# A spectral token mixer: the first transform takes h with rescaled constants, ScalarE copies its whole bank, and the first rows are reordered

## The chip, the cores and the metric

The kernel runs on one core of one Trainium2 chip. The metric is the device time of one execution in microseconds. The core's engines each work through a queue of their own, in order: TensorE (PE, with its weight loads shown apart as PEld), VectorE (DVE), ScalarE (ACT), GpSimd (POOL) and SyncE (SP), which here only issues loads and stores. They meet at semaphores.

## The reference

With x of 2048 tokens by 512 channels, all in float32:

```python
xn = _layernorm(x, axis=-1)
s = _A_ref(xn, A_w_r, A_w_i)      # irfft2(rfft2(xn) * (w_r + 1j * w_i))
g = _silu(_B_ref(xn, B_w1, B_b1, B_w2, B_b2))
return x + s * g
```

`_B_ref` normalises xn once more to h, and mixes the tokens of each channel: gelu(h^T w1 + b1) w2 + b2, with 1792 hidden units, transposed back. So one branch is a two-dimensional spectral filter, the other a token MLP, and the gated product is added to x.

## The kernel before

The 2048 tokens lie as 16 rows of 128 (token 16p + j is partition p of row j), so that row j is one 128x512 tile. The work falls into three stages: up to about 107 us the rows are normalised, the first half of the hidden units is accumulated, and the first transform is made; up to about 217 us the other half of the hidden units and the filter; then w2, the inverse transforms and the output. The change lies in the first stage, in a loop over j from 0 to 15.

**What a row needs.** The mean and the variance of each token come from `stats` and `spreads` (L165, L175, L169, L170), a square root on ScalarE (L171), and `scales` (L179 to L183), which end in `nb`, the bias with which ScalarE makes h. Rows are done in pairs: one set of these small operations serves two rows, except at rows 0 and 1, which have sets of their own. There are two scales for each token, columns 0 and 1 of `rs`: the first makes xn of x, the second makes h of x directly, for the second normalisation of an already normalised token is one more scale.

- h (L186, ScalarE, `normed`) is split into a high part `hh` (L311, `high`, ScalarE) and the remainder `hl` (L314, `low`, VectorE), so that a product in float32 becomes three products of rounded parts. Rows of w1 are split in the same way, 4 blocks of 128 units (`w1h`, `w1l`, 128x512) and 3 blocks (128x384).
- PE then adds 7 x 3 products of 512 columns to banks 0 to 6 (L319, `hidden_early`).
- xn (L189, VectorE, `normed_v`) goes through the first transform: 4 products with the constants `cf` (L197, `first_transform`) into bank 7, between the second and the third group of row products. The tokens of the row are the contracted dimension.
- `first_copy` (L202) brings the second half of bank 7 to SBUF, and `fold` adds and subtracts the first half from PSUM (L207, L208), makes the combinations `t` (L210, L211), moves half of `o` to the other partitions by ScalarE (L215), and writes `ey` by VectorE (L218) and POOL (L213, L214).

**What sets the order.** Operations within `keep(...)` stay on their engine in the order in which the program writes them; this holds for all that VectorE and ScalarE do in this loop. PE's, POOL's and SP's instructions are placed by the scheduler. In iteration j the program writes row j's products, then the preparation of row j + 1 (h, splits), then the fold of row j, and in even iterations the moments of rows j + 2 and j + 3, so that ScalarE and VectorE work one row ahead of PE. In ScalarE's queue the copy of o (L215) of row j stands directly ahead of h of row j + 2.

**Buffers.** h has one buffer, xn two, x five; raw w1 three in each of its two pools. SP issues the loads in the order written, except where a load must wait for a buffer or a queue.

Of the kernel before, what the change touches and what calls it, by code (L numbers as in the profile page):

```python
# [15 lines left out]
P = 128  # L16
# [90 lines left out]
def spectral_mixer_kernel(tc, x, w1, b1, w2, b2, wk, we, wx, c_f, c_ft, c_d, c_i, c_g, c_h, out):  # L107
# [14 lines left out]
    with tc.tile_pool(name="ps", bufs=1, space=PSUM) as psp, ExitStack() as left, ExitStack() as right:  # L122
# [28 lines left out]
        def load_x(j):  # L151
            xs[j] = lnp.tile([P, D], F32, name=f"x{j}", tag="x", bufs=5)
            SY.dma_start(xs[j], x[:, j])
# [3 lines left out]
        def moments(nm, n):  # L157

            return {k: lnp.tile([P, 2, w], F32, name=f"{k}{nm}", tag="m" + k, bufs=3)[:, :n]
                    for k, w in (("st", 6), ("mv", 2), ("v2", 2), ("sd", 2), ("r0", 2), ("t", 2), ("rs", 2), ("nb", 1))}

        def stats(m, i, src):
            keep(V.bn_stats(m["st"][:, i], src))  # L165
# [12 lines left out]
        def scales(m):  # L178
# [4 lines left out]
            keep(V.scalar_tensor_tensor(m["nb"], m["mv"][:, :, 0:1], -1.0, m["rs"][:, :, 1:2], op0=ALU.mult, op1=ALU.mult))  # L183

        def normed(dst, src, m, i):
            keep(A.activation(dst, src, AF.Identity, bias=m["nb"][:, i], scale=m["rs"][:, i, 1:2]))  # L186
# [4 lines left out]
        def new_h(j):  # L191
            return lnp.tile([P, D], F32, name=f"h{j}", tag="h", bufs=1)

        def first_transform(xn):
            z = ps[:, 7].rearrange("p (b c) -> p b c", c=P)
            for b in range(4):
                T.matmul(z[:, b], xn[:, b * P:(b + 1) * P], cf, start=True, stop=True)  # L197
            return z

        def first_copy(j, z):  # L200
            zt = lnp.tile([P, 2, P], F32, name=f"zt{j}", tag="zt")
            keep(A.activation(zt, z[:, 2:4], AF.Copy))  # L202
            return zt

        def fold(j, z, zt):
            e, o, t = (lnp.tile([P, w, P], F32, name=f"{n}{j}", tag=n) for n, w in (("e", 2), ("o", 2), ("t", 1)))
            yield keep(V.tensor_sub(o, z[:, 0:2], zt))  # L207
            yield keep(V.tensor_add(e, z[:, 0:2], zt))  # L208

# [91 lines left out]
        raws = {(0, 0): w1_load(0, *WA)}  # L301
        SY.dma_start(cf, c_f)
        load_x(1)
        raws[0, 1] = w1_load(0, *WB)
        for j in range(2, 5):
            load_x(j)
        for _ in range(WARM):
            T.matmul(ps[:, 0], wz[:, :P], wz, start=True, stop=True)

        def high(dst, src):  # L310
            keep(A.activation(dst, src, AF.Copy))  # L311

        def low(dst, src, hi):
            keep(V.tensor_sub(dst, src, hi.bitcast(F32)))  # L314
# [10 lines left out]

        def new_xn(j):
            return lnp.tile([P, D], F32, name=f"xn{j}", tag="xn")

        m = moments("m0", 2)
# [5 lines left out]
        w = w1_tiles(0, *WA), w1_tiles(0, *WB)  # L335
        h, xn = new_h(0), new_xn(0)
# [16 lines left out]
        folds = iter(())  # L353
        for j in range(NJ):
            more = j + 1 < NJ
            if more:
                raws[j + 1, 0], raws[j + 1, 1] = w1_load(j + 1, *WA), w1_load(j + 1, *WB)
            if j == 0:
                SY.dma_start(b1t, b1)
                SY.dma_start(b2t, b2)  # L360
                G.dma_start(cft, c_ft)
            if j == 4:
                SY.dma_start(cd, c_d)
            if j in (6, 8, 10, 12):
                q = slice(16 * (j - 6), 16 * (j - 4))
                SY.dma_start(out[q, :NJ - 1], x[q, :NJ - 1])
            z = hidden_early(j, 4, 0, w[0], lambda: first_transform(xn))
            hidden_early(j, 3, 4, w[1], lambda: None)
            if more:
                w = w1_tiles(j + 1, *WA), w1_tiles(j + 1, *WB)  # L370
                h, xn = new_h(j + 1), new_xn(j + 1)
# [12 lines left out]
            if j + 3 < NJ:  # L384
# [394 lines left out]
```

## Time and profile before

| | |
|---|---|
| time, median of 3 runs | 400.4 us (400.11 to 401.9) |
| profiled execution | 400.3 us, its span 398.5 us |
| PE busy, share of span | 387.5 us, 97% |
| DVE | 333.9 us, 84% |
| ACT | 238.4 us, 60% |
| POOL | 49.3 us, 12% |
| first stage | 0 to about 107 us |

The span runs from the first to the last instruction that the profiler saw; 1.8 us of the profiled execution lie around it. A busy share counts time in which an engine has an instruction in work, and matmuls are pipelined with modelled ends, so PE's share says little on whether PE sets the pace. What an engine waited for, and which instruction ended the wait, is read from the groups of instructions and from the chain of waits, which follows the last instruction back from releaser to releaser. In its rows stand the start in us, the length in us, the engine, the tile and the line.

### The profile page before, as it was taken

The page shows a single profiled execution, that of the slowest core. Times are in us where ns is not written, and L with a number is a line of the kernel's source. Part 1 is how long each engine was busy: PE and PEld are TensorE (multiplying, and loading weights), DVE is VectorE, ACT ScalarE, POOL GpSimd, SP SyncE. Part 2 cuts the span into 40 slices and gives each one's busy share as a digit, 9 for nine tenths or more (in the row PEclk, how much of TensorE's full clock was granted, in tenths as well). Part 3 has the DMA queues.
Part 4 walks back from the last instruction along what each step waited for, and adds up shares of the span by engine and source line. Part 5 has one row for each costly group of instructions (what it writes and reads, how often), then busy time and mean ns, then how long its engine had stood idle before and what let it go on. Part 6 is the DMA issues. An engine that isn't in the chain of part 4 may idle for free.

```text
span 398.5 us, 7090 instructions
## 1 busy us (share of the span) xinstructions
PE 387.5 (97%) x2456; PEld 337.5 (85%) x2456; DVE 333.9 (84%) x792; ACT 238.4 (60%) x439; POOL 49.3 (12%) x90
## 2 busy tenths in 40 slices
PE   8989999999999999999999999999999999999995
PEld 4677777778877878787878889999999999999995
DVE  5888888988789989998889599888887878787964
ACT  3445444455887875678775677474746465655552
POOL 1111212212200000000000101221210211020200
PEclk9999999999999999999999999999999999999999
DMA  7836344721563645566344839979787878795602
GB/s 249 286 127 200 118 158 159 259 66 39 139 204 128 184 130 172 157 174 177 115 126 146 211 102 260 204 222 178 215 162 204 149 217 147 213 157 156 117 16 53
DMA packets 35080, 64.72 MB, mean 162 GB/s; under 512 B 4194, under 2 KB 19426, under 8 KB 34916
## 3 DMA queue, kind: packets, MB, share of 16 engines
q1 hardware_dynamic: 30436, 52.86, 42.7%
q0 software_dynamic: 4608, 11.41, 17.5%
q8 instruction: 19, 0.31, 0.3%
q14 instruction: 17, 0.14, 0.1%
HBM read 60.05 MB, written 8.13 MB: 171 GB/s over the span
## 4 chain that ended last, share of the span: by engine, by line
PE 69%; DVE 17%; ACT 6%; DMA 5%; issue 2%; SPq 1%; DVEq 0%; ACTq 0%; POOLq 0%
PE ps L717 33%; PE ps L119 6%; PE ps L118 6%; PE ps L120 6%; PE ps L319 4%; PE ps L652 4%; PE ps L421 3%; PE ps L429 3%; DVE w1l L314 3%; PE ps L480 3%; ACT h L186 2%; DMA s<-in_w_dram 2%; DMA w1r<-in_w_dram 2%; DVE stm L165 2%; DVE h L314 2%
## 5 line engine op out<-in xcount | busy, mean ns | idle before, releaser
L319 PE MATMUL ps<-h,w1h 128*128 128x512 f32 x224 | 60.7, 402 | 2.4 <-ACT h L311 2.0
L319 PEld LDWEIGHTS ps<-h,w1h 128*128 128x128 f32 x224 | 40.6, 189 | 12.6 <-ACT h L311 3.6
L118 PE MATMUL ps<-h,w1h 128*128 128x512 f32 x112 | 50.4, 451 | 0.1
L596 DVE TENSOR_TENSOR w2f<-s,w2f 128x896 fp32r<-128x896 f32 x32 | 34.9, 1092 | 17.7 <-ACT w2f L595 17.0
L120 PE MATMUL ps<-h,w1l 128*128 128x512 f32 x112 | 45.3, 404 | 0.0
L119 PE MATMUL ps<-h,w1h 128*128 128x512 f32 x112 | 44.3, 395 | 0.0
L717 PE MATMUL ps<-fa,w2f 128*128 128x256 f32 x336 | 43.1, 281 | 0.0
L717 PE MATMUL ps<-fb,w2f 128*128 128x256 f32 x336 | 42.8, 281 | 0.1
L717 PE MATMUL ps<-fc,w2f 128*128 128x256 f32 x336 | 41.4, 280 | 0.9 <-DVE fc L258 0.9
L717 PEld LDWEIGHTS ps<-fa,w2f 128*128 128x128 f32 x336 | 41.2, 188 | 0.8 <-DVE w2f L596 0.2
L717 PEld LDWEIGHTS ps<-fb,w2f 128*128 128x128 f32 x336 | 40.8, 188 | 0.7 <-DVE c L687 0.5
L717 PEld LDWEIGHTS ps<-fc,w2f 128*128 128x128 f32 x336 | 40.0, 188 | 1.3 <-DVE fc L258 1.1
L595 ACT ACTIVATE w2f<-s 128x896 fp32r<-128x896 f32 x32 | 30.2, 949 | 15.9 <-DVE s L609 11.2
L319 PE MATMUL ps<-h,w1l 128*128 128x512 f32 x112 | 31.4, 394 | 0.0
L596 DVE TENSOR_TENSOR w2f<-a,w2f 128x896 fp32r<-128x896 f32 x24 | 26.1, 1086 | 5.4 <-ACT w2f L595 5.4
L595 ACT ACTIVATE w2f<-a 128x896 fp32r<-128x896 f32 x24 | 22.8, 949 | 11.2 <-PE ps L717 7.9
L586 POOL DMA_DIRECT2D s<-in_w_dram x16 | 13.8, 861 | 115.3 <-DMA s<-in_w_dram 44.3
L314 DVE TENSOR_TENSOR w1l<-w1r,w1h 128x512 fp32r<-128x512 f32 (+1 forms) x32 | 19.8, 620 | 9.0 <-ACT w1h L311 9.0
L118 PEld LDWEIGHTS ps<-h,w1h 128*128 128x128 f32 x112 | 21.2, 189 | 6.3 <-issue 2.6
L119 PEld LDWEIGHTS ps<-h,w1h 128*128 128x128 f32 x112 | 21.2, 189 | 5.6 <-issue 2.6
L120 PEld LDWEIGHTS ps<-h,w1l 128*128 128x128 f32 x112 | 21.0, 188 | 5.4 <-issue 1.0
L319 PEld LDWEIGHTS ps<-h,w1l 128*128 128x128 f32 x112 | 21.0, 188 | 4.9
(123 smaller groups left out, 776.0 us busy)
## 6 DMA issues: line engine op xcount, KB each, us to landing
a<-in_w_dram SPq DMA_DIRECT2D x24, 448.0 KB, 3.8
wt<-in_wk_dram SPq DMA_DIRECT2D x16, 512.0 KB, 3.7
s<-in_w_dram SPq DMA_DIRECT2D x16, 448.0 KB, 4.3
s<-in_w_dram POOLq DMA_DIRECT2D x16, 448.0 KB, 6.5
w1s<-in_w_dram SPq DMA_DIRECT2D x48, 128.0 KB, 2.7
w1r<-in_w_dram SPq DMA_DIRECT2D x16, 256.0 KB, 4.0
x<-in_x_dram SPq DMA_DIRECT2D x15, 256.0 KB, 3.1
out_dram<-in_x_dram SPq DMA_DIRECT2D x4, 960.0 KB, 7.9
```

Of the source, the lines that this page charges most:

```text
L118: T.matmul(o, lh, rh, start=first, stop=False)
L119: T.matmul(o, lh, rl, start=False, stop=False)
L120: T.matmul(o, ll, rh, start=False, stop=last)
L314: keep(V.tensor_sub(dst, src, hi.bitcast(F32)))
L319: T.matmul(ps[:, bank + i], w[wi][:, i * P:(i + 1) * P], hj, start=first and j == 0, stop=last and j == NJ - 1)
L421: T.matmul(pd[:, b * P:(b + 1) * P], eyl[:, b], cd[:, b], start=True, stop=True)
L429: T.matmul(px, gf, sh, start=True, stop=True)
L586: G.dma_start(t, w2_half(*added), accum_op=ALU.add)
L595: A.activation(wf[:, 0], v, AF.Copy)
L596: V.tensor_sub(wf[:, 1], v, wf[:, 0].bitcast(F32))
L652: T.matmul(pe[:, b % 2, b // 2], yt[:, b], ci[:, b], start=True, stop=True)
L717: T.matmul(o, wf[:, wi, i], ui, start=m + a == 0 and n in (1, 2, 5), stop=m == NH - 1 and a == 2, skip_group_check=n in (6, 3, 7, 4))
```

## The change

xn is no longer made. The two scales of a token differ by a factor q, which is the first scale over the second; POOL computes it as `rs0 * rs1 * v2` by two small multiplications per set of scales. Since the tokens are the contracted dimension, xn's transform is h's with row p of the constants multiplied by q of token p: ScalarE makes such constants for each row (`turned`, 128x128), and the transform takes h and these. For rows from 2 on the program writes the transform ahead of the row's products. `first_copy` takes the whole bank, and the fold reads SBUF alone. h gets two buffers, t one. On ScalarE the high part of h now comes ahead of w1h, then the constants, the copy of z, and the smaller w1h. At the start, row 1's statistics stand within row 0's preparation, x of row 1 is loaded ahead of the constants, x of rows 3 and 4 behind w1 of row 1, and the load of cft is written in iteration 4.

```diff
-                    for k, w in (("st", 6), ("mv", 2), ("v2", 2), ("sd", 2), ("r0", 2), ("t", 2), ("rs", 2), ("nb", 1))}
+                    for k, w in (("st", 6), ("mv", 2), ("v2", 2), ("sd", 2), ("r0", 2), ("t", 2), ("rs", 2), ("nb", 1),
+                                 ("q", 1))}
...
+            G.tensor_mul(m["q"], m["rs"][:, :, 0:1], m["rs"][:, :, 1:2])
+            G.tensor_mul(m["q"], m["q"], m["v2"][:, :, 1:2])
+
...
         def new_h(j):
-            return lnp.tile([P, D], F32, name=f"h{j}", tag="h", bufs=1)
-
-        def first_transform(xn):
+            return lnp.tile([P, D], F32, name=f"h{j}", tag="h")
+
+        def turned(j, m, i):
+
+            c = lnp.tile([P, P], F32, name=f"cf{j}", tag="cfj")
+            keep(A.activation(c, cf, AF.Copy, scale=m["q"][:, i]))
+            return c
+
+        def first_transform(h, c):
             z = ps[:, 7].rearrange("p (b c) -> p b c", c=P)
             for b in range(4):
-                T.matmul(z[:, b], xn[:, b * P:(b + 1) * P], cf, start=True, stop=True)
+                T.matmul(z[:, b], h[:, b * P:(b + 1) * P], c, start=True, stop=True)
             return z
...
-            zt = lnp.tile([P, 2, P], F32, name=f"zt{j}", tag="zt")
-            keep(A.activation(zt, z[:, 2:4], AF.Copy))
+            zt = lnp.tile([P, 4, P], F32, name=f"zt{j}", tag="zt")
+            keep(A.activation(zt, z, AF.Copy))
             return zt
...
-            e, o, t = (lnp.tile([P, w, P], F32, name=f"{n}{j}", tag=n) for n, w in (("e", 2), ("o", 2), ("t", 1)))
-            yield keep(V.tensor_sub(o, z[:, 0:2], zt))
-            yield keep(V.tensor_add(e, z[:, 0:2], zt))
+            e, o, t = (lnp.tile([P, w, P], F32, name=f"{n}{j}", tag=n, bufs=w) for n, w in (("e", 2), ("o", 2), ("t", 1)))
+            yield keep(V.tensor_sub(o, zt[:, 0:2], zt[:, 2:4]))
+            yield keep(V.tensor_add(e, zt[:, 0:2], zt[:, 2:4]))
...
         raws = {(0, 0): w1_load(0, *WA)}
-        SY.dma_start(cf, c_f)
         load_x(1)
         raws[0, 1] = w1_load(0, *WB)
-        for j in range(2, 5):
-            load_x(j)
+        SY.dma_start(cf, c_f)
+        load_x(2)
...
         normed(h, xs[0], m, 0)
+        m1 = moments("m1", 1)
+        stats(m1, 0, xs[1])
         low(w[0][1], raws[0, 0], w[0][0])
+        spreads(m1, 1)
         high(w[1][0], raws[0, 1])
-        normed_v(xn, xs[0], m, 0, 0)
+        c = turned(0, m, 0)
         low(hl[0], h, hh[0])
+        scales(m1)
         low(w[1][1], raws[0, 1], w[1][0])
-        m = moments("m1", 1)
-        stats(m, 0, xs[1])
-        spreads(m, 1)
-        scales(m)
-        of = {1: (m, 0)}
+        of = {1: (m1, 0)}
...
             if j == 0:
+                load_x(3)
+                load_x(4)
                 SY.dma_start(b1t, b1)
                 SY.dma_start(b2t, b2)
-                G.dma_start(cft, c_ft)
             if j == 4:
                 SY.dma_start(cd, c_d)
+                G.dma_start(cft, c_ft)
...
-            z = hidden_early(j, 4, 0, w[0], lambda: first_transform(xn))
+            if j > 1:
+                z = first_transform(h, c)
+                hidden_early(j, 4, 0, w[0], lambda: None)
+            else:
+                z = hidden_early(j, 4, 0, w[0], lambda: first_transform(h, c))
             hidden_early(j, 3, 4, w[1], lambda: None)
             if more:
...
                 normed(h, xs[j + 1], *of[j + 1])
+                high(hh[j + 1], h)
                 high(w[0][0], raws[j + 1, 0])
-                high(hh[j + 1], h)
-                normed_v(xn, xs[j + 1], *of[j + 1], 0)
+                c = turned(j + 1, *of[j + 1])
+                zt = first_copy(j, z)
+                high(w[1][0], raws[j + 1, 1])
                 low(w[0][1], raws[j + 1, 0], w[0][0])
-                high(w[1][0], raws[j + 1, 1])
                 if j == 0:
                     stats(m, 0, xs[2])
                 low(hl[j + 1], h, hh[j + 1])
+            else:
+                zt = first_copy(j, z)
             if j + 5 < NJ:
                 load_x(j + 5)
-            zt = first_copy(j, z)
...
-            folds = fold(j, z, zt)
+            folds = fold(j, zt)
```

How the order of instructions moves is shown at three places. The number behind a name tells one tile from another; h_87, h_89 and h_90 are the rounded parts of rows 0, 2 and 3, and h with a higher number is h itself. Lines of the changed kernel stand 9 to 13 lower (L314 becomes L323, L218 becomes L228).

First ScalarE, from the z copy of row 1 to the preparation of row 3. Before:

```order
L202 ACTIVATE zt_322<-ps 128x256
L215 ACTIVATE o_327<-o_327 64x128
L186 ACTIVATE h_371<-x_117,nbm_195,rsm_194 128x512
L311 ACTIVATE w1h_3_367<-w1r_3_338 128x512
L311 ACTIVATE h_90<-h_371 128x512
L311 ACTIVATE w1h_3_369<-w1r_3_340 128x384
L202 ACTIVATE zt_382<-ps 128x256
```

And now:

```order
L212 ACTIVATE zt_326<-ps 128x512
L320 ACTIVATE w1h_2_318<-w1r_2_289 128x384
L225 ACTIVATE o_336<-o_336 64x128
L190 ACTIVATE h_380<-x_203,nbm_197,rsm_196 128x512
L320 ACTIVATE h_90<-h_380 128x512
L320 ACTIVATE w1h_3_376<-w1r_3_347 128x512
L201 ACTIVATE cf_384<-cf,qm_198 128x128
L212 ACTIVATE zt_386<-ps 128x512
L320 ACTIVATE w1h_3_378<-w1r_3_349 128x384
```

In both, the copy of o stands ahead of h. Behind h came w1h of 4 blocks, then the high part of h, the smaller w1h, and the copy of z; now the high part comes second, w1h third, and the constants and the copy of z stand between w1h and the smaller w1h.

Then VectorE at the same place, from the end of the scales of rows 2 and 3 to t of row 1. Before:

```order
L183 SCALAR_TENSOR_TENSOR nbm_195<-mvm_189,rsm_194 128x2
L218 SCALAR_TENSOR_TENSOR ey<-t_255,o_254 128x16x8 x2
L189 TENSOR_SCALAR xn_312<-x_115,mvm_189,rsm_194 128x512
L314 TENSOR_TENSOR w1l_2_308<-w1r_2_278,w1h_2_307 128x512
L314 TENSOR_TENSOR h_89<-h_311,h_89 128x512
L165 BN_STATS stm_265<-x_119 128x6
L314 TENSOR_TENSOR w1l_2_310<-w1r_2_280,w1h_2_309 128x384
L207 TENSOR_TENSOR o_327<-ps,zt_322 128x256
L208 TENSOR_TENSOR e_326<-ps,zt_322 128x256
L210 TENSOR_TENSOR t_328<-o_327 64x128
L211 TENSOR_TENSOR t_328<-o_327 64x128
```

And now:

```order
L184 SCALAR_TENSOR_TENSOR nbm_197<-mvm_191,rsm_196 128x2
L228 SCALAR_TENSOR_TENSOR ey<-t_261,o_260 128x16x8 x2
L323 TENSOR_TENSOR w1l_2_317<-w1r_2_287,w1h_2_316 128x512
L323 TENSOR_TENSOR h_89<-h_320,h_89 128x512
L166 BN_STATS stm_273<-x_205 128x6
L323 TENSOR_TENSOR w1l_2_319<-w1r_2_289,w1h_2_318 128x384
L217 TENSOR_TENSOR o_336<-zt_326 128x256
L218 TENSOR_TENSOR e_335<-zt_326 128x256
L220 TENSOR_TENSOR t_337<-o_336 64x128
L221 TENSOR_TENSOR t_337<-o_336 64x128
```

xn is gone from ahead of w1l; w1l, which reads w1h, is the first operation behind the two ey, and hl follows it as before.

Last VectorE at the start, from behind row 0's high part on. Before, up to row 1's bias:

```order
L189 TENSOR_SCALAR xn_156<-x_105,mvm_138,rsm_143 128x512
L314 TENSOR_TENSOR h_87<-h_155,h_87 128x512
L314 TENSOR_TENSOR w1l_0_154<-w1r_0_113,w1h_0_153 128x384
L165 BN_STATS stm_170<-x_111 128x6
L175 BN_AGGR mvm_171<-stm_170 128x2
L169 TENSOR_SCALAR v2m_172<-mvm_171 128x1
L170 TENSOR_SCALAR v2m_172<-mvm_171 128x1
L179 RECIPROCAL r0m_174<-sdm_173 128x2
L180 TENSOR_TENSOR tm_175<-r0m_174 128x2
L181 SCALAR_TENSOR_TENSOR tm_175<-tm_175,v2m_172 128x2
L182 SCALAR_TENSOR_TENSOR rsm_176<-tm_175,r0m_174 128x2
L183 SCALAR_TENSOR_TENSOR nbm_177<-mvm_171,rsm_176 128x1
```

And now, up to row 0's smaller w1l:

```order
L166 BN_STATS stm_163<-x_110 128x6
L323 TENSOR_TENSOR w1l_0_149<-w1r_0_108,w1h_0_148 128x512
L176 BN_AGGR mvm_164<-stm_163 128x2
L170 TENSOR_SCALAR v2m_165<-mvm_164 128x1
L171 TENSOR_SCALAR v2m_165<-mvm_164 128x1
L323 TENSOR_TENSOR h_87<-h_152,h_87 128x512
L180 RECIPROCAL r0m_167<-sdm_166 128x2
L181 TENSOR_TENSOR tm_168<-r0m_167 128x2
L182 SCALAR_TENSOR_TENSOR tm_168<-tm_168,v2m_165 128x2
L183 SCALAR_TENSOR_TENSOR rsm_169<-tm_168,r0m_167 128x2
L184 SCALAR_TENSOR_TENSOR nbm_170<-mvm_164,rsm_169 128x1
L323 TENSOR_TENSOR w1l_0_151<-w1r_0_112,w1h_0_150 128x384
```

The statistics of row 1 now stand ahead of w1l of row 0, the small operations around hl of row 0, and the smaller w1l of row 0 behind them; xn of row 0 is gone.

PE's transform of a later row, written first in its row, stands in PE's order behind the first four products (of w1h with the high part of h), ahead of those of w1l. POOL's load of cft, written in iteration 4, stands in POOL's order where it stood, ahead of all multiplications.

More of the change, by code (lines that the diff above doesn't have):

```diff
@@ L324, in hidden_early @@
             return r
-        def new_xn(j):
-            return lnp.tile([P, D], F32, name=f"xn{j}", tag="xn")
         m = moments("m0", 2)
@@ L335, in spectral_mixer_kernel @@
         w = w1_tiles(0, *WA), w1_tiles(0, *WB)
-        h, xn = new_h(0), new_xn(0)
+        h = new_h(0)
         high(w[0][0], raws[0, 0])
@@ L370, in spectral_mixer_kernel @@
                 w = w1_tiles(j + 1, *WA), w1_tiles(j + 1, *WB)
-                h, xn = new_h(j + 1), new_xn(j + 1)
+                h = new_h(j + 1)
                 normed(h, xs[j + 1], *of[j + 1])
+                high(hh[j + 1], h)
                 high(w[0][0], raws[j + 1, 0])
-                high(hh[j + 1], h)
-                normed_v(xn, xs[j + 1], *of[j + 1], 0)
+                c = turned(j + 1, *of[j + 1])
+                zt = first_copy(j, z)
+                high(w[1][0], raws[j + 1, 1])
                 low(w[0][1], raws[j + 1, 0], w[0][0])
-                high(w[1][0], raws[j + 1, 1])
                 if j == 0:
```

3 lines of the change are left out of this document (1 added, 2 removed).

## The prediction

> **What bounds the kernel now.** I read the waits of the stage first, then the chain of waits, then the order of time on ScalarE. The chain says which loop sets the pace; the waits say how much slack the others have.
>
> The span, then the stretch from 19 to 93 us (busy time of PE, PEld, DVE, ACT and POOL), and the two waits that recur in every row there (total us, times, longest):
>
> ```profile
> span 398.5 us, 7090 instructions
> ```
>
> ```profile
> 19.00:93.00 74.00, 70.60 (x343) 55.59 (x342) 63.98 (x189) 35.58 (x79) 12.32 (x24) 1.00 0.46 149
> ```
>
> ```profile
> ACT o L215 <- DVE t L211: 26.3, 12, 2.7
> ...
> DVE w1l L314 <- ACT w1h L311: 6.0, 12, 0.6
> ```
>
> Busy shares alone don't find the limit: PE is busy 70.6 of 74 us, VectorE 64.0. But VectorE idles twelve times, 6.0 us in all, for ScalarE's high half of w1, and ScalarE waits twelve times for the second combination t (L211). Two engines that wait for each other once a row form a loop. Here is one turn of it in the chain of waits (start us, us, what), from one h to the next:
>
> ```profile
> 18.95 0.82 ACT h L186
> ...
> 20.31 0.56 DVE w1l L314
> ...
> 20.92 0.68 DVE h L314
> 21.61 0.60 DVE stm L165
> 22.21 0.46 DVE w1l L314
> 22.67 0.34 DVE o L207
> 23.00 0.34 DVE e L208
> ...
> 23.36 0.29 DVE t L210
> ...
> 23.67 0.47 DVE t L211
> ...
> 24.16 0.32 ACT o L215
> ...
> 24.49 0.82 ACT h L186
> ```
>
> No PE row stands in it. The turn takes 24.49 - 18.95 = 5.54 us: ScalarE makes h and the high half of w1 (w1h), VectorE then works through its row as far as t, ScalarE copies a half of o, and only behind that copy comes the next h. Rows whose turn also holds the aggregates and the scales (L175 to L183) take longer. The ends of the run of turns, and the end of the stage on PE:
>
> ```profile
> 92.75 0.82 ACT L186 ACTIVATE h<-x,nbm,rsm 128x512 f32<-128x512 f32 x1 [0.74 <-DVE nbm L183]
> ...
> 97.70 0.81 ACT L186 ACTIVATE h<-x,nbm,rsm 128x512 f32<-128x512 f32 x1
> ...
> 100.10 1.79 PE L319 MATMUL ps<-h,w1h 128*128 128x512 f32 x7
> ...
> 106.55 0.40 PE L118 MATMUL ps<-h,w1h 128*128 128x512 f32 x1
> ```
>
> From 18.95 (row 2's h) to 92.75 (row 14's) there are twelve turns in 73.80 us, 6.15 each. A row of PE itself takes less: the group at 100.10 holds row 14's last 3 matmuls and row 15's first 4, so row 15 begins 3/7 of the way to 101.73, the next group, near 100.80, and it ends where L118 starts, at 106.55: 5.75 us. PE waits for the loop, by about 0.4 us a row.
>
> **The change, part by part.**
>
> *ScalarE's order in a row.* Now, with durations, in row 2:
>
> ```profile
> 19.67 0.61 ACT L311 ACTIVATE w1h<-w1r 128x512 fp32r<-128x512 f32 x1
> 20.19 0.61 ACT L311 ACTIVATE h<-h 128x512 fp32r<-128x512 f32 x1
> 20.71 0.51 ACT L311 ACTIVATE w1h<-w1r 128x384 fp32r<-128x384 f32 x1
> 21.12 0.36 ACT L202 ACTIVATE zt<-ps 128x256 f32<-128x256 f32 x1
> ```
>
> Independent copies start 0.10 us before their predecessor's end (19.67 against 18.95 + 0.82 = 19.77; 20.19 against 20.28). The wait of VectorE ends when w1h is done: 20.31 is 1.36 after h's start. The change puts the high half of h ahead of w1h, and VectorE's first operation of the row is still w1l. The high half reads the h just written, so it can't overlap it: it starts at h + 0.82 + a gap. For this gap the chain has 0.01 to 0.03 us (o's copy, 24.16 + 0.32, to h, 24.49; t's end, 23.67 + 0.47, to o's copy); I take 0.03, so 0.85. w1h follows 0.52 later, as 20.19 to 20.71 does, at 1.37, lasts 0.61, and VectorE starts 0.03 behind it, at h + 2.01 instead of 1.36. **Each turn grows by 0.65 us.** The bounds: 0.52 if the dependent copy overlapped as an independent one does, 0.80 if the gap were 0.18.
>
> *What VectorE no longer does.* xn is 0.54 us a row, but it stands outside the chain: it runs while VectorE would wait for w1h anyway. So it is worth nothing here; its absence makes that wait longer, from 0.50 on average to about 0.50 + 0.54 - 0.1 + 0.65 = 1.6 us. The fold reads both operands from the z copy in SBUF instead of one from PSUM:
>
> ```profile
> L189 DVE TENSOR_SCALAR xn<-x,mvm,rsm 128x512 f32<-128x512 f32 x16 | 8.7, 542 | 0.0
> ...
> L207 DVE TENSOR_TENSOR o<-ps,zt 128x256 f32<-128x256 f32 x16 | 6.7, 417 | 0.0
> ...
> L423 ACT ACTIVATE sh<-ps 128x512 f32<-128x512 f32 x7 | 4.1, 592 | 0.9 <-PE ps L421 0.9
> ...
> L450 DVE TENSOR_TENSOR pq<-xc 128x256 f32<-128x256 f32 x4 | 1.7, 418 | 0.0
> ...
> L454 POOL TENSOR_TENSOR s<-zi,e 128x2 f32<-128x2 f32 x5 | 1.4, 280 | 25.9 <-ACT zi L432 10.0 <-DVE fa L258 5.8 <-DVE r L451 5.3
> ```
>
> Same size, 417 ns from PSUM and 418 from SBUF: nothing.
>
> *What ScalarE gains.* The copy of the whole bank takes 592 ns (L423, the same shape) for 360, and the rescaled constants (128x128) are not in the trace: between o's copy, 0.31 us, and that plus 0.20, the excess of h with its two per-row operands (0.82) over w1h (0.61). Both lie between w1h and the smaller w1h. With the upper bound the smaller w1h ends at h + 1.98 + 0.41 + 0.49 + 0.41 = 3.29, and VectorE wants it after w1l, h and the statistics, 22.21 - 20.31 = 1.90 later than 2.01, at 3.91. Covered by 0.6 us, 0 on the path; without the cover (rows 14 and 15 have no statistics, 0.6 less) it would just touch. PE may start row j with four products of w1h, ahead of the transform, so the constants don't hold it back. Copying all of z also frees bank 7 earlier; PE's waits for it lie in the 0.4 us that PE has over.
>
> *The two multiplications on POOL* cost 280 ns each (L454, same kind). They start when the scales do end, and the constants are wanted 1.9 us later: covered. They could hurt in another way, on the port. Here POOL's ey and VectorE's t run together:
>
> ```profile
> 23.41 0.56 POOL L213 TENSOR_TENSOR ey<-e 128x128 f32<-128x128 f32 x1 [5.23 <-DVE e L208]
> 23.67 0.46 DVE L211 TENSOR_TENSOR t<-o 64x128 f32<-64x128 f32 x1
> ```
>
> The t that meets POOL takes 0.46 us, the same-sized one before it 0.29 (the chain's 23.36 row). nb, which h waits for, follows rs on VectorE as closely as t follows e in the chain (23.00 + 0.34 to 23.36: 0.02), while POOL's ey began 0.07 after e ended, so nb should win: 0 taken, 0.17 as upper bound, in six turns, 1.0 us.
> The Trainium skill (SBUF — State Buffer, Who interferes with whom) states that a VectorE instruction with two SBUF inputs and a GpSimd instruction that reads SBUF exclude each other for a whole instruction. The 0.46 us agrees in direction; by that rule nb could lose a whole POOL multiplication per pair of rows, six times 0.28, and the sum would be 1.7 us higher.
>
> *The start.* Row 1's statistics come before row 0's last splits, and x of row 1 is loaded in the place of the constants:
>
> ```profile
> 2.13 0.43 SPq L302 DMA_DIRECT2D cf<-in_c_f_dram  x1
> 2.60 0.43 SPq L153 DMA_DIRECT2D x<-in_x_dram  x1
> ...
> 9.15 0.68 DVE L165 BATCH_NORM_STATS2 stm<-x 128x6 f32<-128x512 f32 x1
> 9.87 0.18 DVE L175 BATCH_NORM_AGGREGATE mvm<-stm 128x2 f32<-128x6 f32 x1
> ...
> 10.33 0.20 ACT L171 ACTIVATE sdm<-v2m 128x2 f32<-128x2 f32 x1 [2.16 <-DVE v2m L170]
> ...
> 11.36 0.16 DVE L183 SCALAR_TENSOR_TENSOR nbm<-mvm,rsm 128x1 f32<-128x1 f32 x1
> ...
> 11.60 0.82 ACT L186 ACTIVATE h<-x,nbm,rsm 128x512 f32<-128x512 f32 x1 [1.07 <-DVE nbm L183]
> ```
>
> x of row 1 is issued at 2.13 instead of 2.60. Today its statistics run at 9.15 because they stand behind VectorE's other work. A load of x lands 3.1 us after its issue in the median:
>
> ```profile
> x<-in_x_dram SPq DMA_DIRECT2D x15, 256.0 KB, 3.1
> ```
>
> So x of row 1 is there at 5.3, or some two us later among the crowd of first loads; moved up, the statistics start at about 6.5 (6.0 to 7.2); w1l (0.61) 7.8, aggregate to square root takes 10.33 - 9.87 + 0.20, say 8.5, with hl (0.69) in between until 8.85; from square root to h is 11.60 - 10.53 = 1.07 now: **row 1's h starts at 10.0** (9.6 to 10.4) instead of 11.60. Row 2's h follows after 18.95 - 11.60 + 0.65 = 8.0, at 18.0, against 18.95: 0.95 gained. The loads of x 3 and x 4 go behind w1 of row 1 on SP's queue: x 3 is six issues behind x 1, at 0.47 us each (2.13 to 2.60) 5.0, and wanted at 10.0 + 2.01 + 1.8 = 13.8: covered, as are the constants, two issues behind x 1 and wanted near 9. POOL's load of cft keeps its place in POOL's order.
>
> *The sum.* Row 14's h: 18.0 + 73.80 + 12 x 0.65 = 99.6. Row 14 starts when its w1h is done, 101.6; row 15's h follows 97.70 - 92.75 + 0.65 = 5.6 later, its w1h at 107.2, when PE is just through row 14 (101.6 + 5.75 = 107.35). Row 15 ends at 113.1 instead of 106.55: +6.55. What ScalarE does next comes late too:
>
> ```profile
> 103.73 0.39 ACT L202 ACTIVATE zt<-ps 128x256 f32<-128x256 f32 x1 [0.44 <-PE ps L197]
> ...
> 105.43 0.69 ACT L252 ACTIVATE u<-ps,b1t 128x512 f32<-128x512 f32 x1
> ```
>
> Today the last z copy starts 2.8 us before the end of row 15 and the first gelu 1.1 us before it. After the change that z copy stands behind o's copy of row 14, which ends at 105.2 + 5.6 = 110.8; with 0.6 for z, 0.64 for a w1 copy and 1.3 for the table the first gelu starts at 113.3 and ends at 114.0, where the next stage's second group wants its bank at 113.1 + 0.7 = 113.8: +0.2 (0 to 1.5). All that follows is PE, or loads whose buffers come free at the end of a stage, and moves along. 400.3 (the profiled execution: span 398.5 and 1.8 around it, 0.1 under the median of 400.4) + 6.55 + 0.2 = **407.0 us**.
>
> **The rivals.**
>
> *VectorE's share decides (faster).* If 0.54 us less on VectorE counted in full, a turn would drop from 6.15 to PE's 5.75, 0.40 x 12 = 4.8, with the 0.95 of the start 394.6. For it: VectorE's 64 of 74 us, and h with a second buffer. It would need h to begin ahead of o's copy, where ScalarE idles 2.7 us; but ScalarE's queue keeps o's copy first. It decides if VectorE's wait before w1l vanishes. The Trainium skill (Perfetto Trace Analysis, Identifying the Most-Contended Engine) says to optimise the engine with the highest occupancy first, which speaks for this rival; the trace's 6.0 us of waits on that engine speak against. Chance 0.07.
>
> *The turns stay as they are (no change).* If w1h were ready in time by other means, only the start counts: 400.3 - 0.95 = 399.4. It needs VectorE to find work ahead of w1l; the order shows none but the two ey. Chance 0.06.
>
> *The scalars come late (slower still).* POOL delays nb (1.0 us in all), or its first multiplication, behind an instruction that the trace gives no time for, delays row 0's constants, and with them row 1's h, which stands behind them on ScalarE: up to the 1.6 us that the start would have gained, 0.95 of it on the path. Together 408 to 409. It decides from the point where a multiplication ends later than w1h. Chance 0.08.
>
> *The forecast* has 0.79. Its own range: with 0.52 a turn 1.6 less, with 0.80 1.8 more, the start 0.4 either way, ScalarE's lag up to 1.3 more: 404.5 to 410. To hold 8 in 10 with the two faster cases mostly outside I widen it to **403 to 410.5**. A measurement of this kernel tells about 0.5% from no change. Faster by more than that: 0.07. Within it: 0.06. Slower: 0.79 + 0.08 = 0.87.
>
> **What would show it.** In the profile after, VectorE's w1l should wait some 1.6 us in each row for w1h, 19 us over the twelve turns; h starts should lie 6.2 and 7.4 us apart in turn; row 1's h should start near 10.0 and row 15 end near 113; no time should appear between w1h and h's products on PE. I am wrong if the h starts stay 6.15 apart on average, if ScalarE runs h ahead of o's copy, or if the end of row 15 lies before 107.

## The result and the profile after

The change made the kernel slower: 410.04 us in the median of four runs (409.1 to 410.37) against 400.25 (399.96 to 401.9) of the kernel before beside it, a ratio of 1.0235 [1.021, 1.0261]. The profiled execution took 409.83 us with a span of 408.1, against 400.3 and 398.5.

In the changed kernel h is L190, a high part L320, a remainder L323, the rescaled constants L201, the z copy L212, t L220 and L221, the copy of o L225, row products L328 and the transform L207. The first view is the busy time in the stretch from 19 to 93 us (PE, PEld, DVE, ACT, POOL), then the waits from 19 to 102 us (total us, times, longest):

```profile
19.00:93.00 74.00, 65.29 (x318) 52.33 (x319) 52.96 (x155) 38.85 (x82) 13.87 (x32) 1.00 0.45 145
```

```profile
ACT o L225 <- DVE t L221: 26.5, 12, 2.7
DVE w1l L323 <- ACT w1h L320: 20.8, 13, 1.7
...
PE ps L328 <- ACT w1h L320: 10.9, 13, 1.5
```

VectorE is busy for 53.0 of 74 us, where it was 64.0, and the time grew all the same. What it saved, and more, is now idle time in front of w1l: 20.8 us over 13 rows, 1.6 each, against 6.0 over 12 from 19 to 93 us before. PE's products wait for the same w1h, 10.9 us in all.

One turn in the chain of waits after, from row 2's h to row 3's (start us, us, what):

```profile
17.34 0.83 ACT h L190
...
18.19 0.63 ACT h L320
18.82 0.53 ACT w1h L320
...
19.38 0.04 DVE w1l L323
...
19.99 0.62 DVE h L323
20.60 0.67 DVE stm L166
21.27 0.46 DVE w1l L323
...
23.23 0.31 ACT o L225
...
23.56 0.83 ACT h L190
```

Against the chain before there is one piece more, ScalarE's high half of h (18.19), between h and w1h. The turn takes 23.56 - 17.34 = 6.22 us instead of 5.54. The ends of the run of turns, and of the stage, in the order of time:

```profile
31.03 0.81 ACT L190 ACTIVATE h<-x,nbm,rsm 128x512 f32<-128x512 f32 x1 [0.69 <-DVE nbm L184]
...
98.99 0.81 ACT L190 ACTIVATE h<-x,nbm,rsm 128x512 f32<-128x512 f32 x1 [0.69 <-DVE nbm L184]
...
113.02 0.39 PE L118 MATMUL ps<-h,w1h 128*128 128x512 f32 x1
```

Twelve turns take 98.99 - 17.34 = 81.65 us, 6.80 each instead of 6.15; row 15 ends at 113.02 instead of 106.55. What follows is the hand-over, by which I mean the time from there to the first spectrum copy (sh, L436; L423 before). Before, on ScalarE:

```profile
102.66 0.63 ACT L115 ACTIVATE w1h<-w1s 128x512 fp32r<-128x512 f32 x1
...
104.13 1.28 ACT L252 ACT_TABLE_LOAD   x1
...
109.98 0.62 ACT L423 ACTIVATE sh<-ps 128x512 f32<-128x512 f32 x1
```

After, ScalarE, with one row of PE:

```profile
110.24 0.60 ACT L212 ACTIVATE zt<-ps 128x512 f32<-128x512 f32 x1
111.95 0.63 ACT L115 ACTIVATE w1h<-w1s 128x512 fp32r<-128x512 f32 x1 [1.11 <-DMA w1s<-in_w_dram]
112.60 1.28 ACT L262 ACT_TABLE_LOAD   x1
113.90 0.69 ACT L262 ACTIVATE u<-ps,b1t 128x512 f32<-128x512 f32 x1
...
118.32 0.62 ACT L436 ACTIVATE sh<-ps 128x512 f32<-128x512 f32 x1
```

```profile
114.64 0.50 PE L118 MATMUL ps<-h,w1h 128*128 128x512 f32 x1 [0.77 <-ACT u L262]
```

The hand-over is 109.98 - 106.55 = 3.43 us before and 118.32 - 113.02 = 5.30 after: 1.87 more. From sh to the end of the span it is 288.5 before and 289.8 after. So the difference of the spans, 408.1 - 398.5 = 9.6 us, is 6.47 from the first stage (6.55 foretold), 1.87 from the hand-over (0.2 foretold), and 1.3 behind it (nothing foretold).

### The profile page after: what moved, and what is told of

Read it like the earlier page. It is cut to its first block, busy times and chain, and to the rows that moved or that the text cites. A ratio compares the mean times of both kernels' runs of the same rounds, so it can differ in the third digit from the quotient of the medians.

```text
span 408.1 us, 7109 instructions
## 1 busy us (share of the span) xinstructions
PE 388.4 (95%) x2456; PEld 337.9 (83%) x2456; DVE 327.0 (80%) x776; ACT 247.8 (61%) x455; POOL 54.2 (13%) x108
## 4 chain that ended last, share of the span: by engine, by line
PE 54%; DVE 22%; ACT 12%; DMA 7%; issue 4%; SPq 0%; POOL 0%; DVEq 0%; ACTq 0%; POOLq 0%
PE ps L730 26%; PE ps L119 6%; PE ps L118 5%; PE ps L120 5%; PE ps L434 3%; PE ps L442 3%; DVE w1l L323 3%; ACT h L190 3%; PE ps L493 3%; PE ps L665 3%; DMA s<-in_w_dram 2%; ACT h L320 2%; DVE h L323 2%; DVE stm L166 2%; ACT w1h L320 2%
## 5 line engine op out<-in xcount | busy, mean ns | idle before, releaser
L328 PE MATMUL ps<-h,w1h 128*128 128x512 f32 x224 | 61.0, 399 | 10.9 <-ACT w1h L320 10.9
L328 PEld LDWEIGHTS ps<-h,w1h 128*128 128x128 f32 x224 | 40.8, 188 | 24.6 <-ACT w1h L320 16.4
L608 ACT ACTIVATE w2f<-s 128x896 fp32r<-128x896 f32 x32 | 30.1, 948 | 15.9 <-DVE s L622 11.2
L323 DVE TENSOR_TENSOR w1l<-w1r,w1h 128x512 fp32r<-128x512 f32 (+1 forms) x32 | 19.9, 620 | 23.9 <-ACT w1h L320 23.9
L328 PE MATMUL ps<-h,w1l 128*128 128x512 f32 x112 | 31.9, 401 | 0.0
L120 PEld LDWEIGHTS ps<-h,w1l 128*128 128x128 f32 x112 | 21.0, 188 | 5.4 <-issue 1.0
L225 ACT ACTIVATE o<-o 64x128 f32<-64x128 f32 x16 | 4.9, 309 | 31.4 <-DVE t L221 31.4
```

The source lines that it names most:

```text
L120: T.matmul(o, ll, rh, start=False, stop=last)
L328: T.matmul(ps[:, bank + i], w[wi][:, i * P:(i + 1) * P], hj, start=first and j == 0, stop=last and j == NJ - 1)
L608: A.activation(wf[:, 0], v, AF.Copy)
```

## The experiments

The theory is that the loop between ScalarE and VectorE sets the pace of the first stage, and the place of hh ahead of w1h lengthens every turn; the rivals are that VectorE's load decides, or that another part of the change costs the time. A second question is the hand-over. "Pair" is two turns, an even row and an odd one. Each ratio is against runs of the kernel before on the same chip.

| kernel | median us | ratio [95%] | us a turn | row 15 ends | hand-over |
|---|---|---|---|---|---|
| before (beside the change) | 400.25 | 1 | 6.15 | 106.55 | 3.43 |
| the change | 410.04 | 1.0235 [1.021, 1.0261] | 6.80 | 113.02 | 5.30 |
| change, w1h first again | 399.49 | 0.9986 [0.9969, 1.0004] | 6.14 | 104.09 | 3.87 |
| before, swap alone | 410.14 | 1.0239 [1.0208, 1.027] | 6.82 | 114.64 | 3.44 |
| change, VectorE's hl first | 403.25 | 1.0074 [1.0048, 1.01] | 6.29 | 106.17 | 4.42 |
| change, w1h first, late copy | 393.81 | 0.983 [0.9795, 0.9865] | 5.56 | 99.16 | 3.27 |
| change, hh first, late copy | 398.02 | 0.9939 [0.9918, 0.996] | 5.90 | 101.93 | 4.58 |
| before, no xn | 400.47 | 1.0009 [0.9992, 1.0025] | 6.12 | 106.01 | 3.38 |
| before, late copy | 397.12 | 0.9904 [0.9878, 0.993] | 5.74 | 102.43 | 3.31 |
| change, four raw buffers | 405.72 | 1.013 [1.0112, 1.0147] | 6.80 | 112.94 | 3.56 |
| before, four raw buffers | 399.27 | 0.997 [0.9953, 0.9987] | 6.15 | 105.92 | 3.46 |
| change, w1h first, late copy, four raw buffers | 391.65 | 0.9788 [0.9752, 0.9825] | 5.56 | 98.83 | 3.26 |

### The swap undone, and the swap alone

The change with w1h ahead of hh again:

```diff
                 normed(h, xs[j + 1], *of[j + 1])
-                high(hh[j + 1], h)
                 high(w[0][0], raws[j + 1, 0])
+                high(hh[j + 1], h)
                 c = turned(j + 1, *of[j + 1])
```

> The changed kernel with one pair of ScalarE's operations put back: the high half of w1 ahead of the high half of h, in every row. All else of the change stays. Loop theory (each turn grew by 0.65 us because VectorE's first operation waits for w1h, which stood one dependent copy later): the twelve turns from row 2's h to row 14's fall from 6.80 to 6.15 us, row 2's h starts near 16.7, row 15 of PE ends near 104 instead of 113.0, and since PE then has the last rows in arrear, the hand-over to the next stage (from row 15's end to the first copy of the spectrum) falls from 5.3 to about 3.4 us: 397 to 399.5 us in all. New-work theory (the larger copy of z, the constants, the fold out of SBUF and POOL's multiplications cost the time): the turns stay near 6.8, 408 to 410 us.

The kernel before with that one swap and nothing else:

```diff
                 normed(h, xs[j + 1], *of[j + 1])
-                high(w[0][0], raws[j + 1, 0])
                 high(hh[j + 1], h)
+                high(w[0][0], raws[j + 1, 0])
                 normed_v(xn, xs[j + 1], *of[j + 1], 0)
```

> The kernel before, with only that pair exchanged: the high half of h ahead of the high half of w1. Loop theory: turns of 6.80 us instead of 6.15, row 14's h near 101.2 instead of 92.75, hand-over near 5.3 us, 408 to 411 us, though nothing of the change's new work is in it. New-work theory: 400.3 us, as before.

Row 2's and row 14's h with the swap undone, and then with the swap alone (ScalarE in order of time):

```profile
16.45 0.82 ACT L190 ACTIVATE h<-x,nbm,rsm 128x512 f32<-128x512 f32 x1 [0.69 <-DVE nbm L184]
...
90.17 0.81 ACT L190 ACTIVATE h<-x,nbm,rsm 128x512 f32<-128x512 f32 x1 [0.69 <-DVE nbm L184]
```

```profile
18.86 0.81 ACT L186 ACTIVATE h<-x,nbm,rsm 128x512 f32<-128x512 f32 x1 [0.74 <-DVE nbm L183]
...
100.64 0.82 ACT L186 ACTIVATE h<-x,nbm,rsm 128x512 f32<-128x512 f32 x1 [0.74 <-DVE nbm L183]
```

73.72 and 81.78 us for twelve turns: 6.14 and 6.82. The swap alone gives the whole loss (1.0239 against the change's 1.0235), and without it the rest of the change comes out even (0.9986). That settles which edit it is.

The equal ratios are made up differently, though. With the swap alone row 15 ends 8.1 us later than before (114.64 for 106.55), and the hand-over stays at 3.44 us, where I had expected about 5.3. In the change the earlier start takes 1.6 us off the first stage and the hand-over puts 1.87 on. So the longer hand-over needs both: it is 3.43 before, 3.44 with the swap alone, 3.87 with the rest of the change alone, and 5.30 with the two together.

The run with the swap undone also shows that xn, the bank copy, the constants and the earlier start together are worth nothing that can be measured here, although row 2's h starts 2.5 us earlier than before (16.45 for 18.95). The longer hand-over takes 0.4 of that back, and the profiled execution of this kernel, 398.06 us, is the fastest of its ten, so its trace shows more of a gain than the median bears out.

### What VectorE does first

The change with VectorE's hl ahead of w1l, so that its first operation needs hh, which ScalarE now makes first:

```diff
-                low(w[0][1], raws[j + 1, 0], w[0][0])
-                if j == 0:
-                    stats(m, 0, xs[2])
                 low(hl[j + 1], h, hh[j + 1])
+                low(w[0][1], raws[j + 1, 0], w[0][0])
+                if j == 0:
+                    stats(m, 0, xs[2])
```

> The changed kernel with VectorE's first two operations of a row exchanged: the low half of h, which is ready first, ahead of the low half of w1. ScalarE's order stays that of the change. Loop theory: VectorE starts at h + 1.51 instead of h + 2.01, turns of 6.30 us, 402.5 to 405 us. New-work theory: no different from the changed kernel, 409 to 410 us.

VectorE in row 7 of this kernel:

```profile
48.90 0.69 DVE L323 TENSOR_TENSOR h<-h,h 128x512 fp32r<-128x512 f32 x1 [1.01 <-ACT h L320]
49.51 0.69 DVE L323 TENSOR_TENSOR w1l<-w1r,w1h 128x512 fp32r<-128x512 f32 x1
```

VectorE now waits 1.0 us for hh and none for w1l, and a turn takes 6.29: 0.51 less than in the change, and 0.14 more than before. The remainder has its reason in the two orders: w1h, when it comes first, may overlap h's end and is done 1.33 behind h's start (19.67 + 0.61 against 18.95 in the kernel before); hh doesn't overlap the h that it reads, and is done at 0.85 + 0.63 = 1.48. So what counts is not the order on ScalarE as such, but that it is the order in which VectorE wants the two.

### xn taken away alone

The kernel before, with the transform of h by the plain constants; it leaves out the rescaling of the rows by q, and h has two buffers instead of one:

```diff
-                normed_v(xn, xs[j + 1], *of[j + 1], 0)
...
-            z = hidden_early(j, 4, 0, w[0], lambda: first_transform(xn))
+            t_in = h
+            z = hidden_early(j, 4, 0, w[0], lambda: first_transform(t_in))
```

> The kernel before without xn: the first transform reads h with the plain constants, so the rescaling of each row is left out, and h has two buffers. VectorE loses 0.54 us in each of 16 rows; the order on ScalarE is that of before. Theory of the loop (xn stands in VectorE's wait for w1h): turns 6.15 us (6.05 to 6.2), 399.6 us (398.5 to 400.5). Rival (VectorE's share of the time decides): 12 turns shorter by up to 0.54, 394.6 us (393.5 to 396).

VectorE's wait in it, from 19 to 90 us:

```profile
DVE w1l L314 <- ACT w1h L311: 11.2, 12, 1.0
```

Twelve waits of 11.2 us in all where there were 6.0: 5.2 of the 6.5 us (12 x 0.54) that xn took in this stretch reappear as waiting. The time is 1.0009 [0.9992, 1.0025]. Taking work off VectorE gains nothing while it waits in the same place for ScalarE.

### The loop broken

If the loop sets the pace, then time comes from a turn in which VectorE need not wait for ScalarE. The copy of o and the two ey of odd rows go behind the h, w1h and hh that ScalarE makes in the next iteration, so that those no longer wait for VectorE's t. In the change with w1h first:

```diff
+                next(late, None)
                 c = turned(j + 1, *of[j + 1])
...
                 low(hl[j + 1], h, hh[j + 1])
+                run(late)
...
-            run(folds)
+            if j % 2 == 0 or not more:
+                run(folds)
+            else:
+                late = folds
```

> The first experiment's kernel, and in every second row ScalarE's copy of o (and VectorE's two ey behind it) moved behind the next row's h, w1h and high half of h, so that h no longer waits for VectorE's t in these rows. Loop theory: a pair of turns needs 11.0 us of VectorE and ScalarE, under PE's 11.5 for two rows, so PE sets the pace from row 2 on, row 15 ends near 100 and the whole takes 393 to 396 us. New-work theory, or PE waiting for the copy of z: as the first experiment or slower, 398 us and more.

The h of rows 6, 7 and 8 in this kernel, and VectorE's w1l of rows 6 and 7:

```profile
39.26 0.82 ACT L190 ACTIVATE h<-x,nbm,rsm 128x512 f32<-128x512 f32 x1 [0.69 <-DVE nbm L184]
...
42.21 0.81 ACT L190 ACTIVATE h<-x,nbm,rsm 128x512 f32<-128x512 f32 x1
...
50.38 0.82 ACT L190 ACTIVATE h<-x,nbm,rsm 128x512 f32<-128x512 f32 x1 [0.69 <-DVE nbm L184]
```

```profile
40.63 0.69 DVE L323 TENSOR_TENSOR w1l<-w1r,w1h 128x512 fp32r<-128x512 f32 x1 [1.00 <-ACT w1h L320]
...
44.48 0.84 DVE L323 TENSOR_TENSOR w1l<-w1r,w1h 128x512 fp32r<-128x512 f32 x1
```

The odd row's h comes 2.95 us behind the even one's, its w1l starts with no wait, and a pair takes 11.12 us instead of 12.3. The chain of waits is PE alone from 18.85 us to the end of the stage; a row of it:

```profile
42.46 0.89 PE ps L207 x8
43.35 4.80 PE ps L328 x21
```

PE's row takes 0.89 + 4.80 = 5.69 us, more than the 5.56 of a turn, so PE sets the pace now. The time is 393.81 us, 0.983 [0.9795, 0.9865]: less than both kernels. The same edit in the change's own order, hh first, and in the kernel before, tells what the swap and the rest of the change are worth once one turn in two is free:

> The change with its own order on ScalarE (hh ahead of w1h) and the o copy and ey products of odd rows moved behind the next row's h, hh and w1h. Theory of the loop: the swap costs its 0.65 us only where VectorE waits for w1h, which is now one row in two, so a pair of turns is 11.12 + 0.65 = 11.77 us and 12 turns are 3.9 us longer than with w1h first; 397.7 us (396.5 to 398.7) against 393.8. Rival A (the swap costs 0.65 in every row): 401.6 us (400.5 to 402.5). Rival B (TensorE sets the pace, the swap is free): 393.8 us (393 to 395).

> The kernel before with the late copy alone (o copy and ey of odd rows behind the next row's h, w1h and hh); xn, the constants and the start are those of before. It tells how much of the gain of the late copy needs the rest of the change. Theory: in one row of two VectorE no longer waits for w1h, so there xn's 0.54 us shows: a pair of turns is 11.12 + 0.54 = 11.66 us (5.83 a turn), and 12 turns are 3.8 us shorter than before's 73.8: 396.0 us (395 to 397.5). Rival (the late copy gives all of it without the rest): turns 5.56 us, 393 us (392 to 394.5).

With hh first, row 2's h is at 17.07 and row 14's at 87.84, 11.80 a pair (11.77 expected), and the time is 398.02 (397.7 expected). VectorE's waits from 19 to 90 us in it, and then with w1h first:

```profile
DVE w1l L323 <- ACT w1h L320: 11.6, 7, 1.7
```

```profile
DVE w1l L323 <- ACT w1h L320: 6.4, 7, 1.0
```

Both have seven such waits, one a pair, 1.66 against 0.91 each: the swap costs 0.7 us where VectorE waits for w1h and nothing where it does not. In the kernel before, the late copy gives 397.12, within what was expected (395 to 397.5), though by 11.48 us a pair and not 11.66. From there to 393.81 it is 3.3 us, and row 15 ends 3.3 us earlier too (99.16 instead of 102.43); by ratio, 0.9904 [0.9878, 0.993] against 0.983 [0.9795, 0.9865]. So with the loop broken the rest of the change is worth something. About 2.0 of it stand at row 2's h (16.94 for 18.97), which is the earlier start; what is left comes after, and no run tells xn's part of that from the bank copy's, from the transform's place or from the second buffer of h.

### The hand-over

In the changed order the third piece of w1 for the next stage stands behind row 15's z copy, and its load is late, because SP's issue must wait until VectorE has read row 15's raw w1. The chain of waits of the changed kernel has it so, up to the split at 111.95:

```profile
106.65 0.70 DVE w1l L323
...
107.36 0.33 SPq L506
...
107.74 4.12 DMA w1s<-in_w_dram
```

A fourth raw buffer brings the load forward:

```diff
-            raw = up.tile([P, wide * P], F32, name=f"w1r{f0}_{j}", tag="w1r", bufs=3)
+            raw = up.tile([P, wide * P], F32, name=f"w1r{f0}_{j}", tag="w1r", bufs=4 if up is w1p else 3)
...
-            zt = lnp.tile([P, 4, P], F32, name=f"zt{j}", tag="zt")
+            zt = lnp.tile([P, 4, P], F32, name=f"zt{j}", tag="zt", bufs=1)
...
-            w = w1p.tile([P, 4 * P], F32, name=f"w1s{runs[0][0]}_{j}", tag="w1r", bufs=3)[:, :n]
+            w = w1p.tile([P, 4 * P], F32, name=f"w1s{runs[0][0]}_{j}", tag="w1r", bufs=4)[:, :n]
```

> The change with four instead of three buffers for the raw pieces of w1 (the room comes from a single buffer for zt), so that the third piece for the next stage is loaded before VectorE has finished row 15's w1l, and ScalarE's split of it stands ahead of row 15's z copy again, as in the kernel before. Theory (the 1.9 us that the hand-over grew by are ScalarE's 1.11 us wait for that load plus the split behind it, not the longer turns): turns stay 6.8 us, row 15 ends at 113.0, the table load starts near 110.9 instead of 112.6, and from row 15's end to the first spectrum copy it is 3.6 us (3.4 to 4.0) instead of 5.30; 408.3 us (407.6 to 409.0). Rival (the hand-over grew because of the longer row itself, or because of another order on VectorE): it stays 5.0 to 5.5 and the time 409.5 to 410.4.

ScalarE at the end of the stage in it:

```profile
107.61 1.66 ACT L115 ACTIVATE w1h<-w1s 128x512 fp32r<-128x512 f32 x3
...
110.15 0.60 ACT L212 ACTIVATE zt<-ps 128x512 f32<-128x512 f32 x1
110.77 1.28 ACT L262 ACT_TABLE_LOAD   x1
...
116.50 0.62 ACT L436 ACTIVATE sh<-ps 128x512 f32<-128x512 f32 x1
```

All three pieces are split in one group ahead of the z copy, the table load stands 1.83 us earlier, and the hand-over is 3.56 (expected 3.6) with the same 6.80 us a turn. So the 1.9 us were the late load and the split behind the z copy. (A late load is not the only way: in the kernel with hh first and the late copy the hand-over is 4.58 and no split waits for a load; there the table load at 101.26 stands behind a copy of o that waits 2.54 us for VectorE's t.) But the time fell by 4.3 us and not by 1.8: 405.72, below the range that I had given. In the trace 1.7 of the surplus lie between the first w2 product and the first inverse transform, 7.56 us against the change's 9.23, where PE no longer waits for VectorE's fc. Is that a gain of the buffer itself? The same edit in the kernel before (with a single t too), and in the fastest kernel:

> The kernel before with four buffers for the raw pieces of w1 (room from single buffers for zt and t); nothing else. It tells what part of the gain that the same edit gave on the change (4.3 us, of which 1.8 in the hand-over and 1.7 behind the first w2 product) is a gain of its own. Theory (the edit takes away what the change had made worse in the hand-over, and the rest is an accident of loads in the w2 stage): turns 6.15, hand-over 3.4, 399.6 us (398.5 to 400.5). Rival (the fourth buffer is a gain anywhere, since the loads of w1 in the later stages come earlier too): 398.0 us (397 to 398.4).

> The change with w1h ahead of hh, the late copy in odd rows, and four buffers for the raw pieces of w1 (a single buffer for zt). The hand-over with the late copy alone was 3.27 us and no load was waited for there, so the fourth buffer has nothing to gain in it: 393.5 us (392.5 to 394.3) by the theory. Rival (the fourth buffer is a gain anywhere): 391.8 us (390.8 to 392.4).

The stretch is 7.57 and 7.56 us in them, and 7.56 in the first kernel with the buffer; in the nine kernels without it, it is 8.45 to 10.97. So its shortening belongs to the buffer and is no accident of one execution; I had expected the contrary. In the kernel before the time falls only to 0.997 [0.9953, 0.9987], 0.7 us below the 399.96 beside it and within what the theory had (its profiled execution, 398.17, is again its fastest); on the fastest kernel the median is 391.65, 2.2 below 393.81, as the rival had it, though in another set of runs, and the intervals of the two ratios overlap.

How a raw buffer of w1 shortens a stretch of w2 can be read on ScalarE. The first sum of two pieces of w2 (s, made by a load that adds), in the change and then in the change with four buffers:

```profile
235.77 0.95 ACT L608 ACTIVATE w2f<-s 128x896 fp32r<-128x896 f32 x1 [1.55 <-DMA s<-in_w_dram]
```

```profile
232.09 0.94 ACT L608 ACTIVATE w2f<-s 128x896 fp32r<-128x896 f32 x1
```

In the change ScalarE waits 1.55 us for that sum, and the splits and combinations behind it, up to fc, come late with it: the chain of waits goes from the load of s through this split and VectorE's work to fc. With four buffers there is no such wait, and the chain is PE alone. In SP's queue the loads of w2 stand behind the last loads of w1, which need raw buffers: eight from 217.19 on in the change, six from 215.15 on with four buffers. So s is issued 11.0 us ahead of the first w2 product in the change (225.04 for 236.05) and 13.2 us ahead with four buffers (220.86 for 234.02). All nine kernels without the buffer show a wait for s there, of 0.77 to 3.29 us, and in each the stretch is this wait and 7.68 us, to within 0.01; the three with the buffer show none.

## Why the prediction was right, and where it was not

**The bound.** The loop was the right reading. Two edits, one of VectorE's load alone (no xn: 1.0009) and one of the order alone (swap: 1.0239), separate it from the share of busy time, which the first rival went by.

**The turn.** Foretold: hh at h + 0.85, w1h at 1.37, VectorE at 2.01, so 0.65 more a turn. ScalarE's row 2 after:

```profile
17.34 0.82 ACT L190 ACTIVATE h<-x,nbm,rsm 128x512 f32<-128x512 f32 x1 [0.69 <-DVE nbm L184]
18.19 0.63 ACT L320 ACTIVATE h<-h 128x512 fp32r<-128x512 f32 x1
18.73 0.61 ACT L320 ACTIVATE w1h<-w1r 128x512 fp32r<-128x512 f32 x1
19.25 0.39 ACT L201 ACTIVATE cf<-cf,qm 128x128 f32<-128x128 f32 x1
19.54 0.57 ACT L212 ACTIVATE zt<-ps 128x512 f32<-128x512 f32 x1
20.02 0.51 ACT L320 ACTIVATE w1h<-w1r 128x384 fp32r<-128x384 f32 x1
```

Measured: 0.85, 1.39 and 2.04 (VectorE at 19.38), and 6.80 a turn, 0.65 more. The h starts lie 6.22 (17.34 to 23.56) and 7.47 apart (23.56 to 31.03), as foretold. The lower bound, an overlap of the dependent copy, fell.

**ScalarE's own additions.** The constants take 0.39 us (0.31 to 0.51 foretold), the z copy 0.57 (0.59). The smaller w1h ends at h + 3.19 and VectorE comes to it at h + 3.85 (at 21.19; its row in the chain begins at 21.27, where the statistics end). The cover of 0.6 us was there.

**POOL.** The rows around the scales of rows 2 and 3, in order of time:

```profile
16.95 0.16 DVE L183 SCALAR_TENSOR_TENSOR rsm<-tm,r0m 128x4 f32<-128x4 f32 x1
17.15 0.16 DVE L184 SCALAR_TENSOR_TENSOR nbm<-mvm,rsm 128x2 f32<-128x2 f32 x1
17.19 0.19 POOL L186 TENSOR_TENSOR qm<-rsm 128x2 f32<-128x2 f32 x1 [0.56 <-DVE rsm L183]
...
17.46 0.32 POOL L187 TENSOR_TENSOR qm<-qm,v2m 128x2 f32<-128x2 f32 x1
```

nb starts 0.04 us behind rs's end, ahead of POOL's first multiplication. 0 was right, and the rival of late scalars falls with it: nb loses nothing, and row 0's constants are done at 8.83, ahead of row 1's nb (9.34). The Trainium skill (SBUF — State Buffer, Who interferes with whom) would let nb lose a whole POOL multiplication if POOL came first; here it did not come first. Nor do the records show POOL waiting for nb's end: the two overlap from 17.19 to 17.31 and take 0.19 and 0.16 us. The second multiplication lies nearly wholly beside VectorE's ey (17.23 to 17.73) and took 0.32 us; that ey is the cause is not shown.

**The start.** Row 1's h started at 9.38, earlier than the 9.6 of my best bound; its statistics started at 6.26 (6.5 foretold) and the square root at 7.92, where I had 8.5. The distance to row 2's h, 7.96, was as foretold (8.0). That the whole first stage came out so near (6.47 for 6.55) is in part luck: row 14's h came 0.6 us earlier than foretold (98.99 for 99.6), and from it to the end of row 15 it took 14.0 us instead of 13.5.

**The step that failed is the hand-over: +0.2 where +1.87 was measured.** I had the last z copy behind o's copy, at 110.8 (110.24 measured), and the first gelu at 113.3 (113.90 measured). That the gelu lies so near is luck: the z copy came 0.56 early, and a wait that I didn't have came behind it. Two things were wrong. I didn't ask whether the load for the third piece of w1 would be there, and put down 0.64 for its split alone; the wait for it is 1.11 us. And I counted ScalarE's lateness only from the point where PE wants a bank back, as if the 1.1 us by which the gelu led before were slack. They weren't: sh, which the next stage starts with, stands in ScalarE's own queue behind the table load and six gelus, and between table load and sh there are 5.85 us before (104.13 to 109.98) and 5.72 after (112.60 to 118.32). The table load ran 2.42 us ahead of row 15's end and now runs 0.42 ahead; this loss of 2.0 us went into sh nearly in full. The four-buffer run gave it back (2.17 ahead, hand-over 3.56). My range for the term reached 1.5 and didn't hold it.

**The rest.** I had all that follows move along unchanged. It grew by 1.3 us, of which 0.5 lie between the first w2 product and the first inverse transform (9.23 against 8.72); they are ScalarE's wait for the load of s, 1.55 us for 1.04. The rest of the 1.3 was not traced. Over the kernels run here the time from sh to the end of the span lies between 287.0 and 290.9 us, so a term of about 1 us either way belonged in the range. 407.0 came out 3.0 too low; 410.04 lies in the range to 410.5, but just outside the forecast's own, 404.5 to 410 (its bounds, all taken together, add up to 404.8 and 410.5). The range held it because it had been widened for other reasons, not because it covered the hand-over and what follows.

## What to carry to other kernels

When two engines hand work back and forth once a row, write down the turn from the chain of waits and ask of each edit whether it moves the first thing that the waiting engine needs; work taken off the waiting engine only turns into waiting (no xn: 11.2 us of waits for 6.0, the same time), until the loop is broken, and then the rest of the change, xn's removal in it, brought something (393.81 against 397.12 us). The producer should make things in the order in which the consumer takes them, and a step that depends on its predecessor should not stand between two others. Where an engine runs late into the next stage, its slack is what lies between its last work and the first instruction of its own queue that the next stage needs, not the first moment another engine misses it; and the loads that it waits for belong to that reckoning. Where loads stand in one queue, a load that waits for a buffer also holds up those behind it (the load of s comes 2.2 us later with three buffers than with four).

## What the runs showed of the hardware

A ScalarE copy that reads what the one before has just written starts 0.03 us after that one's end (17.34 + 0.82 to 18.19), where an independent one starts 0.09 before it (18.19 + 0.63 to 18.73): the dependence costs about 0.12 us, which fits the turns of the run with hl first, 0.14 us longer than before. In the late-copy kernel with w1h first VectorE's w1l of four blocks took 0.84 us in each of the seven odd rows from 3 on and 0.69 in each even one. In the odd rows POOL's second ey runs beside its beginning (in row 7 from 44.26 to 44.77, w1l from 44.48), in the even ones no POOL operation does; following another operation at once does not do it, for in the kernel with hl first w1l does so and takes 0.69 (49.51, POOL idle); I had looked for such meetings at the small multiplications, and found one there instead.
